# A dense FFN whose tail is reordered: chunks 0 to 5 of the last three blocks first, then chunks 6 to 15 of all blocks, mostly for 512 tokens at once

## The chip, the core and the metric

The kernel runs on one core of a Trainium2 chip. TensorE (PE, with its weight loads shown apart as PEld), VectorE (DVE), ScalarE (ACT), GpSimd (POOL) and the issuing engine SyncE (SP) each work through their own instructions in order and wait for each other through semaphores. The metric is the time of one execution on the device in microseconds (us); lower is better.

## What is computed

Three layers follow each other on 2304 tokens of 512 features (4 batches of 576):

```python
scores = scale * np.matmul(q, k.transpose(0, 1, 3, 2))      # 8 heads, head size 64
thresh = np.max(scores, axis=-1, keepdims=True) - tau
scores = np.where(scores >= thresh, scores, -1000000000.0)  # softmax over what is left, then @ v
...
h = x @ w_in                        # 512 x 2048
g = np.maximum(0.01 * h, h)
x = (g @ w_out).astype(np.float32)  # 2048 x 512
...
logits = x @ w_gate + modality_bias[modality_id]
e_idx = np.argmax(logits, axis=1)   # one of 8 experts for each token
for e in range(E):
    h = np.maximum(x[mask] @ w1[e], 0.0)
    out[mask] = gate_w[mask, None] * (h @ w2[e])
```

The weights of the dense FFN come as 64-bit floats.

## The kernel before, in words

**Precision by splitting.** Every f32 operand of a large matmul is kept as a high part (rounded to fp32r) and a low part (the rest), and three products are added: high by high, high by low, low by high. `mm1` does the first FFN product for one chunk of 128 hidden features: 4 slices of the 512 inputs, 3 products each, 12 matmuls into one PSUM bank `h`. `leaky` is the activation: ACT copies `h`, DVE takes the maximum, ACT rounds the high part `gh`, DVE subtracts to get `gl`. `mm2` adds the chunk's contribution to the output `y` of 128 tokens: 3 matmuls of 512 columns.

**Blocks, chunks, items.** A block is 256 tokens (`GT`), nine of them; a chunk is 128 of the 2048 hidden features, sixteen of them (`NF`). One block with one chunk is an item: 12 matmuls of 256 columns, a `leaky` on 256 columns, 6 matmuls of 512 columns. The input of a block comes from DRAM (`xd`, written by attention) into the one buffer `ur`, is transposed on PE (`turned`, 8 transposes into two PSUM tiles `tp`) and split by ACT and DVE (`split_x`).

**Weight conversion.** `convs` turns a piece (half a chunk, 128 by 512 double words) into a high and a low tile in four steps: ACT reads the upper words and DVE the lower ones, two more DVE operations put the bits together, then ACT writes the high part and POOL subtracts the low part. The intermediate `s` of the three DVE operations lies in PSUM (tile `cs`) for the first `NBANK` = 9 pieces and in SBUF for the other 23.

**Order of the work.** In the attention stage (16 head pairs with 9 row tiles, 144 steps) PE has room, and `Units` runs partial blocks there: blocks 0 to 5 with chunks 0 to 5 (`FB`, block 0 only chunks 0 to 4), whose sums go to DRAM as `yp` (issued by SP) and are added later. `CV` is the number of conversion steps for each attention step, by quarters of the stage. The partial block of the end also transposes and splits the input of the block that the tail starts with. After attention `un.finish` runs what is left of the units, and then `Tail.run` goes through a list of items: chunks 5 (or 6) to 15 of blocks 0 and 1 interleaved with a shift of two chunks (`AHEAD`), then chunks 6 to 15 of blocks 2 to 5, then all 16 chunks of blocks 6, 7 and 8, then two groups of the mixture of experts (8 items each). `pre` holds what has to be done ahead of an item (fetching an input, its transposes, loading and splitting expert weights). Within each item four conversion steps of `bg` are recorded, and `advance` takes one step of the routing work in `extra`. The matmuls of an item's `mm2` come two items after its `mm1` (`LAG`), and `h` has two banks.

**Routing.** When a block's output is complete (`done1`), the gate logits are computed on DVE (`Route.logits`: 16 fused multiply-and-sum operations of 512 columns a block against broadcast gate weights, which lie in the buffers of the expert weights), for the last block on PE (`logits_mm`: 8 transposes and 16 small matmuls). `Route.block` then finds the expert; five small matmuls `rp` on PE rank the tokens, the rows go to DRAM as `yd`, and POOL scatters the token numbers. `RB` and `LD` say how many calls of `advance` lie between two steps of them. `early` picks the first two expert groups from the blocks routed so far, here seven; their weights may be loaded (`have` = 2) when the eighth block is routed.

```python
RB = [4]*6+[3,3,1]
FB = [5,6,6,6,6,6]
CV = [0.95,0.67,0.67,0.67,0.67]
```

The names that the steps below use: `convs` (L369), `leaky` (L426), `Route.logits` (L533), `logits_mm` (L542), `Route.block` (L560), `Tail.run` (L918), the attention's stores of `xd` (L259, L262), the units' store of `yp` (L1276), the load of a block (L398).

Of the kernel before, what the change touches and what calls it, by code (L numbers as in the profile page):

```python
# [350 lines left out]
class Moe1:  # L351
# [17 lines left out]
    def convs(self, fs, new, tmp, bank, nbank):  # L369
# [7 lines left out]
        for n, (fi, k) in enumerate(seq):  # L377
# [3 lines left out]
            if n < nbank:  # L381
                s = bank().bitcast(I32)
# [31 lines left out]
def mm1(nc, w, x, h):  # L414

    n = 0
    for c in range(4):
# [4 lines left out]
        if c == 1:  # L422
            yield
# [299 lines left out]
class Steps:  # L723
# [9 lines left out]
    def to(self, k):  # L733
        while True:
            next(self)
            if self.n % 4 == k:
                return

# [9 lines left out]
class Tail:  # L748

# [6 lines left out]
    def __init__(self, tc, ctx, mo, rt, un, w1, w2, out, wts):  # L756
# [26 lines left out]
        self.pr = un.ps  # L783
        self.yT = [f(un.ct[i]).rearrange("p (c t) -> p c t", c=4) for i in (2, 0)]
# [14 lines left out]
    def turn(self, key, rows, t):  # L799
        if t == 0:  # L800
            self.xs = self.xh(), self.xl()
        else:
            self.x[key] = self.xs
        tp = self.pr.tile([P, 4, P], F32, tag="u", name="tp")
        turned(self.tc.nc, rows[:, t], tp, self.rt.ident)
        for _ in split_x(self.tc.nc, tp, *self.xs, t):
            pass

    def done1(self, b, ys, part):
        nc = self.tc.nc  # L810
        yt = self.yt()
        for t in range(2):
            if part:
# [9 lines left out]
        if self.blocks < NB:  # L823
# [20 lines left out]
    def load_ids(self, g):  # L844
        assert self.blocks == NB - 2
# [5 lines left out]
    def gather(self, g):  # L851
        xg, ids, rows = self.xgb(), self.idb(), self.rt.yd[0:NT - 2 * GT]
        self.tc.nc.vector.tensor_scalar(ids, self.ids[g], NT - 2 * GT - 1, None, op0=ALU.min)
# [64 lines left out]
    def run(self, items, pre, bg=None):  # L918
# [24 lines left out]
        for n in range(len(items) + self.LAG):  # L943
            if n < len(items):
# [10 lines left out]
                h = self.ph()[:, 0:GT]  # L955
                for _ in mm1(nc, w, self.x[it["x"]], h):
                    for _ in late:
                        pass
                    if bg:
                        bg.to(2)  # L960
                    self.advance()
                if bg:
                    bg.to(3)
                self.advance()
                gs[n] = self.g()
                if it["act"] is relu:
                    relu(nc, h, *gs[n])
                else:
                    late = leaky(nc, h, self.ga(), *gs[n])
# [6 lines left out]
            if n >= self.LAG:  # L976
                it = items[n - self.LAG]
                if it["start"]:
                    ys[it["y"]] = [self.py() for t in range(2)]
                g = gs.pop(n - self.LAG)  # L980
                for t in range(2):
                    mm2(nc, it["wt"], g, ys[it["y"]][t], t, it["start"], it["stop"])
                    if t == 0:
# [4 lines left out]
            if bg:  # L988
                bg.to(0)
# [207 lines left out]
RB = [4]*6+[3,3,1]  # L1197
# [6 lines left out]
FB = [5,6,6,6,6,6]  # L1204
CV = [0.95,0.67,0.67,0.67,0.67]
AHEAD = 2
NBANK = 9
# [3 lines left out]
class Units:  # L1211
# [32 lines left out]
    def block(self, b):  # L1244
# [18 lines left out]
        if b == len(FB) - 1:  # L1263
            yield from self.split(self.part[0])
        for t in range(2):
# [258 lines left out]
```

## Time and profile before

| | |
|---|---|
| median of 3 runs | 1050.35 us (1049.22 to 1051.45) |
| the profiled execution | 1050.26 us, its span 1048.5 us |
| mean granted TensorE clock | 0.963 |
| PE busy / PEld / DVE / ACT / POOL | 89% / 79% / 74% / 57% / 41% of the span |
| attention with units | to about 400 us |
| tail of the FFN, to the first matmul of expert group 0 | about 400 to 768 us |
| expert groups and the rest | 768 us to the end |

The span runs from the first instruction to the last; the execution's own time is 1.76 us more. A row of the timeline gives the start, the busy time, the engine, the line, the operation with out<-in, the count of merged instructions and, in brackets, the idle time before it with what ended it. Matmuls of one row overlap, so the spacing between starts tells how fast PE goes, and the busy time of a row does not.

### The profile page before, as it was taken

What the parts mean: (1) busy time and instruction counts of PE and PEld (TensorE: products, weight loads), DVE (VectorE), ACT (ScalarE), POOL (GpSimd) and SP (SyncE); (2) the same over time, 40 slices, a digit from 0 to 9 for tenths busy, and PEclk for the clock granted to TensorE, in tenths of its full rate; (3) what the DMA queues carried; (4) which work ended last, traced back from release to release, by engine and by line L of the source; (5) the groups of instructions that cost most, each with busy time, mean ns of one, the idle gap of its engine ahead of it and who ended that gap; (6) DMA issues with size and microseconds to landing.
All of it is one profiled execution on the core that took longest, in us unless ns stands there. A gap on an engine that the chain in (4) does not pass through costs nothing. (4 is left out here: it accounts for less than half of the span.)

```text
span 1048.5 us, 21500 instructions
## 1 busy us (share of the span) xinstructions
PE 929.8 (89%) x7409; PEld 827.5 (79%) x7409; DVE 780.8 (74%) x1975; ACT 595.6 (57%) x1234; POOL 430.9 (41%) x514
## 2 busy tenths in 40 slices
PE   4677789989998998778999999999899999999983
PEld 4566678879897997667888888988788998998962
DVE  7998999979898986786777877666458666565573
ACT  6778888878887874443222232322345555564473
POOL 3999999897887862331000000000102211221121
PEclk9888899999999999999999999999989999999997
DMA  8999999999999896444022221100756988665573
GB/s 220 197 241 236 242 238 219 197 212 232 208 186 240 184 180 181 125 156 137 24 62 61 45 37 41 41 22 1 147 196 167 351 292 267 242 234 170 158 262 114
DMA packets 260336, 177.33 MB, mean 169 GB/s; under 512 B 186018, under 2 KB 223014, under 8 KB 260200
## 3 DMA queue, kind: packets, MB, share of 16 engines
q1 hardware_dynamic: 251744, 160.53, 62.7%
q0 software_dynamic: 4736, 12.92, 3.8%
q10 hardware_dynamic: 3720, 2.22, 0.7%
q8 instruction: 65, 1.06, 0.5%
q14 instruction: 71, 0.58, 0.2%
HBM read 115.74 MB, written 18.22 MB: 128 GB/s over the span
## 5 line engine op out<-in xcount | busy, mean ns | idle before, releaser
L452 PE MATMUL y<-w,g 128*128 128x512 f32 x960 | 259.4, 406 | 0.0
L452 PEld LDWEIGHTS y<-w,g 128*128 128x128 f32 x960 | 172.8, 192 | 29.5
L420 PE MATMUL h<-uxh,w 128*128 128x256 f32 x848 | 166.6, 293 | 19.7 <-POOL w L393 7.0
L196 POOL TENSOR_TENSOR p<-p,p 128x512 f16<-128x512 f32 x144 | 169.0, 1173 | 0.0
L420 PEld LDWEIGHTS h<-uxh,w 128*128 128x128 f32 x848 | 137.1, 193 | 33.7 <-DVE g L434 11.9
L150 PE MATMUL s<-khh,qs 128*128 128x288 f32 x320 | 107.3, 348 | 48.5 <-DVE p L175 24.8
L158 DVE TENSOR_REDUCE s<-s 128x1 f32<-128x576 f32 x144 | 109.4, 760 | 29.7 <-PE s L223 26.0
L432 ACT ACTIVATE g<-h 128x256 fp32r<-128x256 f32 x144 | 55.4, 384 | 133.9 <-DVE h L430 131.9
L604 POOL DMA_INDIRECT idt<-ids,pi x18 | 18.7, 1041 | 263.9 <-DVE pi L601 197.9
L420 PE MATMUL h<-uxl,w 128*128 128x256 f32 x424 | 121.3, 286 | 0.7 <-DVE uxl L411 0.7
L175 DVE SCALAR_TENSOR_TENSOR p<-s,tb,e 128x576 f32<-128x576 f32 x144 | 117.3, 815 | 5.6 <-ACT e L167 3.9
L150 PEld LDWEIGHTS s<-khh,qs 128*128 128x128 f32 x320 | 68.1, 213 | 57.8 <-DVE p L175 18.1
L222 PE MATMUL s<-vs,pt 128*128 128x128 bf16 (+1 forms) x680 | 108.5, 227 | 5.7 <-DMA pt<-p 5.7
L428 ACT ACTIVATE ct<-h 128x256 f32<-128x256 f32 x144 | 55.2, 383 | 102.1 <-PE h L420 96.3
L167 ACT ACTIVATE e<-s,tb 128x576 f32<-128x576 f32 x144 | 107.2, 744 | 5.2 <-DVE tb L162 5.2
L223 PE MATMUL s<-vs,pt 128*128 128x64 bf16 (+1 forms) x680 | 103.5, 197 | 0.0
L430 DVE SCALAR_TENSOR_TENSOR h<-h,ct 128x256 f32<-128x256 f32 x144 | 61.7, 429 | 54.5 <-ACT ct L428 53.8
L194 ACT ACTIVATE p<-p 128x576 f16<-128x576 f32 x144 | 99.4, 691 | 3.7 <-DVE kll L111 2.9
L150 PE MATMUL s<-kll,qs 128*128 128x288 f32 x320 | 98.6, 321 | 0.0
L225 PE MATMUL s<-vs,pt 128*128 128x128 bf16 (+1 forms) x544 | 89.1, 225 | 0.0
L420 PE MATMUL h<-exh,w 128*128 128x256 f32 (+1 forms) x448 | 85.8, 287 | 0.7 <-ACT exh L409 0.7
L420 PEld LDWEIGHTS h<-uxl,w 128*128 128x128 f32 x424 | 81.7, 193 | 1.1 <-DVE uxl L411 1.1
(236 smaller groups left out, 2267.7 us busy)
## 6 DMA issues: line engine op xcount, KB each, us to landing
cr<-w SPq DMA_DIRECT2D x36, 512.0 KB, 6.0
raw_qk<-qkt SPq DMA_DIRECT2D x30, 576.0 KB, 5.3
raw<-w SPq DMA_DIRECT2D x24, 512.0 KB, 6.7
eraw<-w SPq DMA_DIRECT2D x18, 512.0 KB, 5.3
cr<-w_in SPq DMA_DIRECT2D x16, 512.0 KB, 4.2
cr<-w_out SPq DMA_DIRECT2D x16, 512.0 KB, 4.2
ur<-xd SPq DMA_DIRECT2D x15, 512.0 KB, 5.1
ur<-w SPq DMA_DIRECT2D x12, 512.0 KB, 3.6
```

The costliest lines, as they stand in the source:

```text
L150: nc.tensor.matmul(s[:, j, 0:288], qf[:, c0:c0 + P], x[:, j * 288:(j + 1) * 288], start=(k == 0), stop=(k == len(ops) - 1))
L158: v.tensor_reduce(self.mq[n], self.sq[n], axis=AX.XY, op=ALU.min)
L167: self.tc.nc.scalar.activation(e, self.sq[n], AF.Exp, bias=self.mq[n][:, 1:2], scale=-1.0)
L175: self.tc.nc.vector.scalar_tensor_tensor(p, self.sq.pop(n), self.mq.pop(n)[:, 0:1], self.eq.pop(n), op0=ALU.is_le, op1=ALU.mult, accum_out ...
L194: nc.scalar.activation(pp[:, 0:S], p, AF.Copy)
L196: nc.gpsimd.tensor_tensor(pp[:, S + D:], p[:, 0:4 * P], pp[:, 0:4 * P], op=ALU.subtract)
L222: nc.tensor.matmul(o[r0:r1, 0:2 * D], hi, v12, start=(c == 0), stop=False)
L223: nc.tensor.matmul(o[r0:r1, D:2 * D], hi, vs[:, h, c, 2], start=False, stop=(c == 4))
L225: nc.tensor.matmul(o[r0:r1, 0:2 * D], pt[:, 5 + c, r0:r1], v12, start=False, stop=False)
L420: nc.tensor.matmul(h, w[:, 0, a, s], b[:, c], start=(n == 0), stop=(n == 11))
L430: nc.vector.scalar_tensor_tensor(h, h, 0.01, a, op0=ALU.mult, op1=ALU.max)
L452: nc.tensor.matmul(y, a[:, s], w[:, 1, b], start=start and k == 0, stop=stop and k == 2)
```

## The change

It reorders the tail, and moves some work into and out of the attention stage:

- Block 0 gets chunk 5 in the attention stage as well (`FB`), and the conversions run faster in its first quarter (`CV` 1.2). The partial block at the end no longer transposes and splits the tail's first input.
- The tail starts with chunks 0 to 5 of blocks 6, 7 and 8 (18 items of 256 tokens), which need no new weights; their sums go to `yp` (`done0`). Then come chunks 6 to 15 of block pairs 0 and 1, 2 and 3, 4 and 5, 6 and 7 with 512 tokens an item (40 wide items; four `y` banks, inputs and activations in the weight tiles of chunks 0 to 5, which are not needed any more), then chunks 6 to 15 of block 8 (10 items).
- Three conversion steps are recorded in an item of 256 tokens and five in a wide one. `s` lies in PSUM until the first wide item, and in SBUF after it.
- The stores of `yp` are issued by ACT, and not by SP. The partial sums of a pair are loaded in the middle of the pair into their own buffers.
- Logits on DVE for the first six blocks only; on PE for the last three. `RB` is 1 for all blocks. `early` and `have` = 2 come after six blocks, and the gather reads only their rows.

```diff
-    def convs(self, fs, new, tmp, bank, nbank):
+    def convs(self, fs, new, tmp, bank):
...
-            if n < nbank:
-                s = bank().bitcast(I32)
+            at = bank()
+            if at is not None:
+                s = at.bitcast(I32)
...
-def mm1(nc, w, x, h):
+def mm1(nc, w, x, h, at=(1,)):
...
-        if c == 1:
+        if c in at:
             yield
...
+        self.x5 = itertools.cycle([[w.rearrange("p a b n -> p (a b) n") for w in wts[2 * i:2 * i + 2]] for i in range(2)]).__next__
+        self.g5 = itertools.cycle([[w[:, i, k] for k in range(2)] for w in wts[4:6] for i in range(2)]).__next__
+        self.a5 = itertools.cycle([f(t) for t in un.ct[0:2]]).__next__
...
+    def done0(self, b, ys):
+
+        for t in range(2):
+            o = f(self.cts[2 * t])
+            self.tc.nc.scalar.activation(o, ys[t], AF.Copy)
+            self.tc.nc.scalar.dma_start(self.mo.yp[2 * b + t], o)
+
+    def fetch_part(self, b):
+        for t in range(2):
+            self.tc.nc.sync.dma_start(self.xgs[b % 2][:, t, 0:DM], self.mo.yp[2 * b + t])
...
+            if part == 2:
+                nc.vector.tensor_tensor(yt[:, t, 0:DM], ys[t], self.xgs[b % 2][:, t, 0:DM], op=ALU.add)
+            elif part:
...
-        if self.blocks < NB:
+        if self.blocks == 1:
+            self.extra.append(iter([None] * 12))
+        if self.blocks <= NB - 3:
             self.extra.append(slowly(self.rt.logits(yt, self.sb, f(self.cts[2])), LD[self.blocks - 1]))
...
-        if self.blocks == NB - 2:
+        if self.blocks == NB - 3:
             self.extra.append(self.rt.early(self.sb1))
-        elif self.blocks == NB - 1:
             self.extra.append(self.routed())
...
-                for _ in mm1(nc, w, self.x[it["x"]], h):
+                if "hook" in it:
+                    it["hook"]()
+                nt = it.get("nt", 2)
+                h = self.ph()[:, 0:nt * P]
+                for _ in mm1(nc, w, self.x[it["x"]], h, (0, 1, 2) if nt == 4 else (1,)):
                     for _ in late:
                         pass
                     if bg:
-                        bg.to(2)
+                        next(bg)
                     self.advance()
...
-RB = [4]*6+[3,3,1]
+RB = [1] * 9
...
-FB = [5,6,6,6,6,6]
-CV = [0.95,0.67,0.67,0.67,0.67]
-AHEAD = 2
-NBANK = 9
+FB = [6,6,6,6,6,6]
+CV = [1.2,0.67,0.67,0.67,0.67]
...
-        if b == len(FB) - 1:
-            yield from self.split(self.part[0])
...
-                nc.sync.dma_start(mo.yp[2 * b + t], self.ys)
+                nc.scalar.dma_start(mo.yp[2 * b + t], self.ys)
...
+        bank[0] = itertools.cycle(ta.pys[2:4]).__next__
         un.finish(cv)
...
+        for b in range(len(FB), NB):
             p = len(items)
...
+            pre += [(p - 5, 0, 0, lambda b=b: ta.fetch(b))] + [(p - 2 + t, 0, 0, lambda b=b, t=t: ta.turn(b, un.xr, t)) for t in range(2)]
+            items += [item(b, fi, start=fi == 0, stop=fi == NA - 1, ys=ta.pys[0:2], done=(lambda ys, b=b: ta.done0(b, ys)))
+                      for fi in range(NA)]
...
+        for b in range(0, NB - 1, 2):
+            p = len(items)
+            for k in range(2):
+                pre += [(p - 4 + 2 * k, 0, 0, lambda b=b, k=k: ta.fetch(b + k)), (p + 5, 0, 0, lambda b=b, k=k: ta.fetch_part(b + k))]
+                pre += [(p - 2 + k, 0, 0, lambda b=b, t=2 * k + t: ta.turn((b,), un.xr, t, True)) for t in range(2)]
+            items += [dict(item(b, fi, start=fi == NA, stop=fi == NF - 1, nt=4, done=(lambda ys, b=b: both(b, ys))), x=(b,))
+                      for fi in range(NA, NF)]
+        items[(NB - len(FB)) * NA]["hook"] = lambda: bank.__setitem__(0, lambda: None)
```

**Where attention ends, on SP.** `xd<-xs` and `xd<-xm` are the attention's last stores, `cr` the raw weights, `ur<-xd` the load of a block's input, `yp<-ct` the units' partial sums. Before:

```order
L1276 DMA yp<-ct_85 128x512
L259 DMA xd<-xs 128x4x128
L262 DMA xd<-xm 64x64 x2
L364 DMA cr_90<-w_in 128x4x256
L1276 DMA yp<-ct_85 128x512
L366 DMA cr_88<-w_out 128x1024
L398 DMA ur<-xd 128x2x512
```

With the change:

```order
L200 DMA_TRANSPOSE pt<-p_138 128x9x128
L259 DMA xd<-xs 128x4x128
L262 DMA xd<-xm 64x64 x2
L364 DMA cr_90<-w_in 128x4x256
L399 DMA ur<-xd 128x2x512
L366 DMA cr_88<-w_out 128x1024
L399 DMA ur<-xd 128x2x512
```

The stores of `yp` are gone from this queue, and the first load of the tail is now block 6, some of whose rows are written by the two stores right ahead of it.

**An item in the middle of the tail, on PE.** Before (`xl` is the low part of the input, `w_7119` and so on a chunk's weights, `y_7109` and `y_7110` the two output banks):

```order
L420 MATMUL h_7106<-xl,w_7119 128x256
L452 MATMUL y_7109<-w_7117,g 128x512 x3
L452 MATMUL y_7110<-w_7117,g 128x512 x3
L420 MATMUL h_7105<-xh,w_7120 128x256 x2
L420 MATMUL h_7105<-xl,w_7120 128x256
```

With the change (`w_70` and `w_71`, once the weights of chunks 2 and 3, hold the input's two parts, and `w_73` an activation):

```order
L421 MATMUL h_7125<-w_71,w_7141 128x512
L453 MATMUL y_7127<-w_7139,w_73 128x512 x3
L453 MATMUL y_7128<-w_7139,w_73 128x512 x3
L453 MATMUL y_7129<-w_7139,w_73 128x512 x3
L453 MATMUL y_7130<-w_7139,w_73 128x512 x3
L421 MATMUL h_7126<-w_70,w_7142 128x512 x2
L421 MATMUL h_7126<-w_71,w_7142 128x512
```

A wide item has as many matmuls of the first product as a narrow one, of twice the columns, and twice as many of the second.

**Routing of a block, on DVE.** `hot` is the one-hot expert, which `rp` on PE reads; `rk` reads `rp`. Before:

```order
L584 TENSOR_TENSOR hot<-w_605,fe 128x16
L434 TENSOR_TENSOR g<-h_7105,g 128x256
L430 SCALAR_TENSOR_TENSOR h_7106<-h_7106,ct_86 128x256
L591 TENSOR_REDUCE g<-ex 128x2
L593 TENSOR_TENSOR rk<-rp,cnt 128x16
```

With the change:

```order
L539 SCALAR_TENSOR_TENSOR ct_87,lw<-yt_91,cr_89 128x512 x2
L539 SCALAR_TENSOR_TENSOR ct_87,lw<-yt_91,cr_90 128x512 x2
L435 TENSOR_TENSOR w_72<-h_7126,w_72 128x512
L572 TENSOR_TENSOR lg<-lw,bsel 128x16
L574 TENSOR_REDUCE mx<-lg 128x2
L577 TENSOR_TENSOR oh<-lg,mx 128x16
L578 TENSOR_TENSOR lg<-lg,mx 128x16
L579 TENSOR_TENSOR oh<-oh,w_612 128x16
L583 TENSOR_REDUCE fe<-oh 128x2
L585 TENSOR_TENSOR hot<-w_612,fe 128x16
L592 TENSOR_REDUCE g<-ex 128x2
L594 TENSOR_TENSOR rk<-rp,cnt 128x16
```

The steps of the routing now follow each other without the activation work of an item between `hot` and `rk`, so the five `rp` matmuls come sooner after `hot` in PE's order.

## Rows read from the trace of the kernel before

**Rows 1.** Stretches: us, busy by engine (x instructions), PEclk, DMA share, GB/s.

```profile
425.00:450.00 25.00, 21.48 (x121) 18.50 (x120) 20.25 (x33) 11.26 (x26) 8.48 (x6) 0.91 0.42 131
450.00:475.00 25.00, 20.26 (x109) 16.94 (x109) 21.26 (x32) 11.05 (x27) 8.49 (x7) 0.91 0.42 139
...
756.00:761.00 5.00, 0.27 (x2) 0.30 (x3) 0.24 (x1) 0.00 (x0) 0.00 (x0) 0.83 0.75 112
761.00:766.00 5.00, 5.00 (x19) 4.42 (x18) 2.23 (x4) 1.91 (x4) 0.00 (x0) 0.50 0.74 269
```

**Rows 2.** Timeline of PE in a stretch without idle time.

```profile
629.50 1.56 PE L452 MATMUL y<-w,g 128*128 128x512 f32 x6
630.90 0.40 PE L420 MATMUL h<-uxh,w 128*128 128x256 f32 x2
...
632.33 1.54 PE L452 MATMUL y<-w,g 128*128 128x512 f32 x6
```

**Rows 3.** Timeline of PE from the end of attention to the first logits.

```profile
400.06 7.21 PE L452 MATMUL y<-w,g 128*128 128x512 f32 x30
407.11 0.40 PE L420 MATMUL h<-uxh,w 128*128 128x256 f32 x2
...
414.73 1.12 PE L404 MATMUL tp<-ident,ur 128*128 128x128 f32 x4 [4.58 <-DMA ur<-xd]
...
424.49 0.39 PE L420 MATMUL h<-uxh,w 128*128 128x256 f32 x1 [1.45 <-POOL w L393]
...
498.44 0.50 PE L420 MATMUL h<-uxh,w 128*128 128x256 f32 x2 [3.46 <-DVE g L434]
```

**Rows 4.** Timeline of PE where expert group 0 begins.

```profile
760.73 1.09 PE L404 MATMUL tp<-ident,xg 128*128 128x128 f32 x4 [5.43 <-DMA xg<-yd,ids]
761.47 2.91 PE L452 MATMUL y<-w,g 128*128 128x512 f32 x6
764.17 0.63 PE L420 MATMUL h<-uxh,w 128*128 128x256 f32 x2
...
766.49 0.60 PE L404 MATMUL tp<-ident,xg 128*128 128x128 f32 x4
...
768.33 0.40 PE L420 MATMUL h<-xh,w 128*128 128x256 f32 x2
```

**Rows 5.** The attention's last output on DVE, then SP's timeline after it.

```profile
400.61 0.28 DVE L254 SCALAR_TENSOR_TENSOR xs<-s,rs,xs 128x64 f32<-128x64 f32 x1 [1.86 <-ACT xs L251]
...
403.76 0.35 SPq L1276 DMA_DIRECT2D yp<-ct  x1
404.24 0.36 SPq L259 DMA_DIRECT2D xd<-xs  x1
404.95 1.10 SPq L262 DMA_DIRECT2D xd<-xm  x2
```

**Rows 6.** Time from issue to landing: the stores of L262, then the loads of L398.

```profile
DMA to landing us min/median/max: 2.1/4.9/7.0
...
DMA to landing us min/median/max: 3.9/5.1/9.6
```

**Rows 7.** Conversion on DVE by line: ns min/median/max; s in PSUM (cs), then SBUF.

```profile
L388 DVE SCALAR_TENSOR_TENSOR cs<-cr,cs x9: 680/684/689, 16.8 to 106.2; 128x512 int32<-128x512 int32 x9
L388 DVE SCALAR_TENSOR_TENSOR yt<-cr,yt x20: 691/1648/1671, 401.3 to 478.8; 128x512 int32<-128x512 int32 x20
```

**Rows 8.** Timeline of DVE while logits run: two starts of the activation, one item apart.

```profile
559.62 0.43 DVE L430 SCALAR_TENSOR_TENSOR h<-h,ct 128x256 f32<-128x256 f32 x1
559.96 0.68 DVE L538 SCALAR_TENSOR_TENSOR ct<-yt,raw 128x512 f32<-128x512 f32 x1
...
562.98 0.43 DVE L430 SCALAR_TENSOR_TENSOR h<-h,ct 128x256 f32<-128x256 f32 x1
```

**Rows 9.** Timeline of PE in the logits of the last block.

```profile
781.00 1.85 PE L557 MATMUL lp<-wg,ct 128*128 128x8 f32 x16
```

**Rows 10.** SP's issues of yp (ns); PE's waits for transposed attention weights, 150 to 400 us.

```profile
L1276 SPq DMA_DIRECT2D yp<-ct x12: 338/444/548, 171.6 to 408.0; - x12
...
PE s L222 <- DMA pt<-p: 4.6, 3, 3.6
```

More of the change, by code (lines that the diff above doesn't have):

```diff
@@ L731, in __next__ @@
         return next(self.gen, None)
[L733 to L737, printed above, removed]
 def slowly(gen, k):
@@ L844, in load_ids @@
     def load_ids(self, g):
-        assert self.blocks == NB - 2
+        assert self.blocks == NB - 3
         base = self.entry(g, 1, NID - GT)
@@ L968, in run @@
                 else:
-                    late = leaky(nc, h, self.ga(), *gs[n])
+                    late = leaky(nc, h, (self.a5 if nt == 4 else self.ga)(), *gs[n])
                     next(late)
@@ L977, in run @@
                 it = items[n - self.LAG]
+                nt = it.get("nt", 2)
                 if it["start"]:
-                    ys[it["y"]] = [self.py() for t in range(2)]
+                    ys[it["y"]] = it["ys"] if "ys" in it else [self.py() for t in range(nt)]
                 g = gs.pop(n - self.LAG)
-                for t in range(2):
+                for t in range(nt):
                     mm2(nc, it["wt"], g, ys[it["y"]][t], t, it["start"], it["stop"])
-                    if t == 0:
+                    if t < nt - 1:
                         self.advance()
@@ L988, in run @@
             if bg:
-                bg.to(0)
+                next(bg)
             self.advance()
@@ L1296, in ev @@
                         self.turn(self.todo[0])
-                    elif b == len(FB) - 1:
-                        self.turn(self.part[0])
                 yield
@@ L1412, in body @@
         ta.sb2 = lambda: groups().sb
+        bank[0] = itertools.cycle(ta.pys[2:4]).__next__
         un.finish(cv)
-        part = un.part
-        full = [b for b in range(NB) if b not in part]
-        jobs = [(b, FB[b]) for b in part[2:]] + [(b, 0) for b in full]
-        def item(b, fi, f0):
-            return dict(x=b, w=(lambda: mo.w[fi]), act=leaky, y=b, start=fi == f0, stop=fi == NF - 1, need=2 * fi + 1,
-                        done=(lambda ys: ta.done1(b, ys, f0 > 0)))
-        b0, b1 = part[:2]
@@ L1422, in body @@
-        two = sorted([(fi, 0, b0) for fi in range(FB[b0], NF)] + [(fi + AHEAD, 1, b1) for fi in range(FB[b1], NF)])
-        items = [item(b, fi - (AHEAD if k else 0), FB[b]) for fi, k, b in two]
-        pre = []
-        ta.x[b0] = un.xh, un.xl
-        ta.xh(), ta.xl()
-        p = [it["x"] for it in items].index(b1)
-        pre += [(p - 9, 0, 0, lambda: ta.fetch(b1))] + [(p - 3 + t, 0, 0, lambda t=t: ta.turn(b1, un.xr, t)) for t in range(2)]
-        for b, f0 in jobs:
-            p = len(items)
-            pre += [(p - 9, 0, 0, lambda b=b: ta.fetch(b))] + [(p - 3 + t, 0, 0, lambda b=b, t=t: ta.turn(b, un.xr, t)) for t in range(2)]
-            items += [item(b, fi, f0) for fi in range(f0, NF)]
+        items, pre = [], []
@@ L1433, in body @@
+        items[(NB - len(FB)) * NA]["hook"] = lambda: bank.__setitem__(0, lambda: None)
+        b, p = NB - 1, len(items)
+        pre += [(p - 4, 0, 0, lambda: ta.fetch(b))] + [(p - 2 + t, 0, 0, lambda t=t: ta.turn((b,), un.xr, t)) for t in range(2)]
+        items += [dict(item(b, fi, start=fi == NA, stop=fi == NF - 1, done=(lambda ys: ta.done1(b, ys, 1))), x=(b,)) for fi in range(NA, NF)]
         p = len(items)
```

28 lines of the change are left out of this document (16 added, 12 removed).

## The prediction

> **What bounds the kernel now.** The stretches come first, since the 89% of the whole span hides them. From 425 to 475 us PE is busy 41.7 of 50 us, at a granted clock of 0.91 [rows 1]: it has work and waits for it. Next, the rate of PE when nothing holds it: an item takes 632.33 - 629.50 = 2.83 us, 1.40 for the six matmuls of `y` and 1.43 for the twelve of `h` [rows 2]; I count 2.82. A matmul of 512 columns so takes 0.233 us and one of 256 columns 0.119: width itself gains nothing on PE. Then the tail against that rate. From its first matmul (407.11) to the first of group 0 (768.33) lie 361.2 us [rows 3, 4]. In it are 109 items less the two `y` parts that come later, 109 x 2.82 - 2.8 = 304.6, and the transposes of nine inputs at 0.44 for four (766.49 to 768.33 is 1.84, less 1.40 for the `y` matmuls between) [rows 4], 7.9. So 48.7 us are lost: at 414.73 to a load (4.58), then to weights in conversion (1.45 at 424.49 is one of twelve such rows to 480), at 498.44 to the first logits (3.46), at 760.73 to the gather for group 0 (5.43) [rows 3, 4]. After an idle stretch PE is slow as well: at 0.50 of the clock, the lower of the two levels, from 761 to 766 [rows 1], the `y` part takes 2.70 for 1.40 and the `h` part 2.32 for 1.41 [rows 4], which with the transposes makes 2.6 us.
>
> The DVE rows say why weights are late: the second operation of a piece takes 1.65 us with `s` in SBUF, 0.68 with it in PSUM [rows 7].
>
> **The change part by part**, as the new time of group 0's first matmul.
>
> *Start of the tail.* The units leave 21 `y` matmuls after attention's last product for the 30 that fill 400.06 to 407.11: 4.9 us, so PE is free at 405.0 [rows 3]. But the first input is now block 6, which needs attention's last stores. Their data are ready at 400.9; SP issues them at 404.24 and 404.95 because the store of `yp` ahead of them waits until 403.76 [rows 5]. Without it the three issues take until 402.5, the last at about 402.0. Landing takes 4.9 (2.1 to 7.0), then the load is issued (0.4) and takes 5.1 (3.9 to 9.6) [rows 6]: 412.4. Transposes 0.88 and, as an estimate, two passes of ACT and DVE over 512 columns at about 0.68 each [rows 7]: first matmul at 414.7. PE is idle for most of 9.7 us, longer than at any place before; I take the 2.6 us of slow clock behind it.
>
> Here a rule speaks against the change. The Trainium skill (DMA: Bandwidth & Descriptors, Issuing engines are not separate DMA queues) says that issuing from several engines saves only the sequencer's time of issue. By it the start would come 3 us later, 417.7. The trace disagrees in that a queue's wait counts as well: 3.3 us passed between ready data and issue [rows 5], so I keep 414.7.
>
> *Narrow items.* 18 x 2.82 = 50.8. Their weights are there already. Conversion goes on at 3 steps, 0.75 pieces, an item: on DVE 0.75 x 3 x 0.68 = 1.5, with 0.43 twice for the activation [rows 8] 2.4 us, under the 2.82 of PE. With `s` in SBUF it would be 0.7 more, over it. For queues that meet I take 2 us; the bounds are 0 and the 12 us lost between 425 and 475 (8.3 idle, and 0.09 of 41.7 to the clock) [rows 1].
>
> *Wide items.* 40 x 5.64 = 225.6, the same PE time as 80 items. One loading buffer serves both blocks of a pair: the second load can start only after the first block's transposes. Before the first pair the two are one narrow item apart, so 5.1 + 0.4 - 2.8 = 2.7 us are lost; at the others a wide item covers it.
>
> *Logits.* On DVE four logits and an activation take 562.98 - 559.62 = 3.36 us [rows 8]. A wide item has room for eight: about 6.5 us of DVE work against 5.64 of PE, for 32 logits in a row instead of 16, after four additions at the pair's end. So DVE falls behind by some 0.9 us an item for two items, beside about 1 from the additions. PE has 8.5 us from a wide `h` to the reuse of its bank, so the activation bears that. The `rp` matmuls don't: they stand in PE's queue one step behind `hot`, where before there were four, and the next items' matmuls are queued behind them. For each of the six blocks I take 1.5 us, 9 in all; bounds 0 (DVE gets there first) and 4 each, all of the lag with the next additions.
>
> *Block 8 and more.* 10 x 2.82 less 2.8 = 25.4. Inputs: eleven more to transpose, and group 0, 12 x 0.88 = 10.6. Two more blocks have logits on PE: 0.88 + 1.85 = 2.7 each [rows 9], 5.4. Rank matmuls 1.8, small waits 1. The gather for group 0 and its weights are ready some items early, since six blocks are enough: the 5.43 us go [rows 4], and so does the wait for the first logits, whose gate weights get 12 steps to arrive.
>
> Sum: 50.8 + 225.6 + 25.4 + 10.6 + 5.4 = 317.8; lost 2.6 + 2 + 2.7 + 9 + 1.8 + 1 = 19.1. From 414.7 this makes 751.6 against 768.33: **-16.7 us**. The groups behind it keep their own work and order, so they count as nothing; what covers them is that their loads start as many items ahead as now.
>
> *Attention.* Nine conversion steps, 2.25 pieces, move from the second quarter to the first: at most +4.6 us (2.25 x 3 x 0.68, all of it on the path), at best -6 (as many pieces at the SBUF price less in the second). Twelve issues of `yp` move to ACT: at most +5.3 (12 x 0.444), at best -4.6, PE's waits for transposes that SP issued late [rows 10]. Block 0's chunk adds 2.8 of PE work, and a split of 0.9 goes; PE idles at the end of each quarter, so 0 to +1.9. I take **+1.5**, in the middle, as the costs and the gains fall on the same engines.
>
> 1050.26 - 16.7 + 1.5 = **1035.0 us**. The profiled execution lies 0.09 us under the median of the runs shown, so nothing is to be corrected.
>
> **The rivals.** (A) *DVE keeps up.* The `rp` cost nothing: 1026. For it: in a pair of 56 us DVE has 10 x 1.4 us of activation and 32 x 0.67 of logits, 35 us, so that it is early again by the pair's end. Against it: the 3.46 at 498.44 shows that logits in the queue do stop PE [rows 3]. (B) *Attention pays.* Both upper bounds, +9.9 instead of +1.5: 1043.4. (C) *Slower: PE stands behind `rp` for whole stretches of logits.* If DVE is late by the work of an item and not by a part of it, each `rp` costs 6.5 us; six make 39 instead of 9: 1065. It decides from 4.4 us each, (9 + 15.3 + 2.1) / 6, the last being the 0.2%. For it: 32 logits in one row, which the kernel before never had. Against it: PE's wait lets DVE catch up, so one long wait shortens the next. (D) *The reordering doesn't free the narrow items:* they still wait on the activation behind conversion, and the 12 us stay: 1045.
>
> **How the numbers follow.** Chances: forecast 0.50, A 0.22, B 0.13, C 0.08, D 0.07. The range goes from A with attention 4 better, 1022, to B with D's half, 1047; C and the worst of B with D lie above it. No change, within 0.2% (2.1 us, about what a measurement of this kernel can tell), needs B and D together or a half of C: 0.06. Slower is C: 0.08. Faster is the rest, 0.86.
>
> **What would show it.** Right: PE busy over 23 of 25 us from about 420 on, at clock 1.00; no wait on POOL or ACT for weights; no gap ahead of group 0's transposes; one gap of 8 to 10 us after attention ended by the load of `ur`; a wait of 2 to 3 us ahead of the first pair; six waits of 1 to 2 us at `rp`. Wrong: `rp` waits over 4 us each; attention's last product later than 406 us; gaps between narrow items; or an idle start much longer than 10 us.

## The result and the profile after

| | before | after |
|---|---|---|
| median of the runs | 1048.58 us (20 runs, 1043.75 to 1051.45) | 1055.68 us (20 runs, 1045.21 to 1063.01) |
| ratio to before, 95% interval | | 1.0052 (1.0027 to 1.0077) |
| profiled execution, its span | 1050.26, 1048.5 us | 1056.48, 1054.8 us |
| mean granted TensorE clock | 0.963 | 0.955 |
| group 0's first matmul | 768.33 | 765.36 |
| from there to the end of the span | 280.2 us | 289.4 us |

The forecast was 1035.0 us, with a range of 1022 to 1047. The kernel became **slower by half a per cent**. The ratio compares the fast runs alone (their means are 1053.9 and 1048.4), without the run of 1063.01, which was in a slower state. The stretches tell where it did what was expected of it, and where not. The windows of the kernel after, with the columns of [rows 1]:

```profile
425.00:450.00 25.00, 23.67 (x153) 21.05 (x152) 19.49 (x39) 15.30 (x35) 7.74 (x6) 1.00 0.52 174
450.00:475.00 25.00, 23.66 (x142) 20.77 (x141) 18.05 (x35) 14.42 (x32) 7.79 (x6) 1.00 0.54 181
475.00:500.00 25.00, 25.00 (x110) 20.27 (x109) 16.89 (x24) 11.81 (x21) 6.76 (x5) 1.00 0.37 127
...
550.00:650.00 100.00, 90.53 (x392) 72.28 (x391) 71.00 (x214) 20.59 (x39) 8.09 (x8) 0.93 0.27 49
...
656.00:662.00 6.00, 5.20 (x17) 4.45 (x18) 1.98 (x3) 1.68 (x3) 0.00 (x0) 0.50 0.01 4
```

The stretch that was bad before, 425 to 475 us, is good now: PE is busy 47.3 of 50 us at full clock, where it was 41.7 at 0.91 [rows 1]. But from 550 us on, where the kernel before had nothing to lose (98.9 of 100 us from 550 to 650, clock 1.00), PE now idles a tenth of the time (busy 90.5 of 100 us) and the mean granted clock is 0.93. The timeline of PE shows each loss:

```profile
399.28 5.12 PE L453 MATMUL y<-w,g 128*128 128x512 f32 x21
409.05 1.67 PE L405 MATMUL tp<-ident,ur 128*128 128x128 f32 x8 [4.65 <-DMA ur<-xd]
411.41 0.80 PE L421 MATMUL h<-uxh,w 128*128 128x256 f32 x2 [0.69 <-ACT uxh L410]
...
466.66 1.07 PE L405 MATMUL tp<-ident,ur 128*128 128x128 f32 x8 [1.34 <-DMA ur<-xd]
...
580.17 0.21 PE L590 MATMUL rp<-hot,tri 128*128 128x8 bf16 x2 [2.64 <-DVE hot L585]
...
617.43 0.20 PE L590 MATMUL rp<-hot,tri 128*128 128x8 bf16 x2 [2.67 <-DVE hot L585]
...
617.57 4.59 PE L453 MATMUL y<-w,w 128*128 128x512 f32 x12
622.00 2.96 PE L421 MATMUL h<-w,w 128*128 128x512 f32 x12
...
656.80 1.94 PE L405 MATMUL tp<-ident,ur 128*128 128x128 f32 x8 [5.04 <-DMA ur<-xd]
...
759.72 1.05 PE L405 MATMUL tp<-ident,xg 128*128 128x128 f32 x4
...
765.36 0.40 PE L421 MATMUL h<-uxh,w 128*128 128x256 f32 x2
...
779.48 1.11 PE L548 MATMUL ytp<-ident,yt 128*128 128x128 f32 x4 [6.82 <-DVE yt L827]
```

Three kinds of wait are new.

**The rank matmuls `rp`.** Six blocks wait 2.43, 2.64, 2.67, 1.73, 2.67 and 1.69 us, 13.8 in all. (A seventh wait, of 1.79 at 757.10, belongs to the fourth pair.) Behind the wait of 2.67 at 617.43 the twelve matmuls of `y` take 622.00 - 617.57 = 4.43 us, where they take 2.80 at full clock. That is 1.6 us more. The first four waits are followed by such a stretch, 6.4 us in all, the last two aren't. With it the six cost 20.2 us. Windows right behind the waits of 580.17, 636.40 and 690.63:

```profile
580.30:583.00 2.70, 2.70 (x11) 2.15 (x10) 1.43 (x8) 0.04 (x1) 0.95 (x1) 0.50 0.84 301
...
636.50:641.00 4.50, 4.50 (x19) 3.56 (x19) 2.22 (x9) 1.19 (x2) 0.96 (x1) 0.67 0.32 118
690.70:695.00 4.30, 4.30 (x23) 3.53 (x24) 3.95 (x16) 0.70 (x2) 0.96 (x1) 1.00 0.66 186
```

**The second input of the fourth pair.** It is waited for 5.04 us at 656.80, and the granted clock behind it is 0.50, the lower of its two levels, in the window of 656 to 662 above: 7.5 us with the 2.5 that this costs the transposes and the `y` matmuls. There was no such wait in this stage before, and the forecast had none here.

**Block 8's partial sums.** At 779.48 PE waits 6.82 us for the output of block 8. SP's issues, and behind them the addition on DVE, tell why:

```profile
759.56 0.38 SPq L880 DMA_DIRECT2D raw<-w  x1
766.11 0.37 SPq L878 DMA_DIRECT2D raw<-w  x1
...
767.20 0.89 SPq L826 DMA_DIRECT2D yt<-yp  x2
```

```profile
778.74 1.41 DVE L827 TENSOR_TENSOR yt<-y,yt 128x512 f32<-128x512 f32 x2 [6.49 <-DMA yt<-yp]
```

The load of `yp` is issued behind two expert weights, one of which stood in the queue until 766.11 for its buffer. It then takes until 778.7 to arrive, while expert weights and, on POOL from 775.05, a token scatter and two gathers are under way. This is the stretch after group 0's first matmul, which the forecast gave nothing.

What DVE does ahead of the `rp` of 580.17:

```profile
577.14 0.18 DVE L572 TENSOR_TENSOR lg<-lw,bsel 128x16 f32<-128x16 f32 x1
...
577.44 0.69 DVE L431 SCALAR_TENSOR_TENSOR h<-h,ct 128x512 f32<-128x512 f32 x1
578.04 1.28 DVE L412 TENSOR_TENSOR w<-tp,w 128x512 fp32r<-128x512 f32 x2
579.24 0.17 DVE L577 TENSOR_TENSOR oh<-lg,mx 128x16 f32<-128x16 f32 x1
...
579.93 0.17 DVE L585 TENSOR_TENSOR hot<-w,fe 128x16 bf16<-128x16 f32 x1
```

The last logit is done at 577.1, before PE came to `rp` (580.17 - 2.64 = 577.53). What PE then waits for here is not logits: it is an activation and the split of the next pair's first input, 1.7 us, and a chain of small operations, 0.9, which all stand ahead of `hot` in DVE's order. Read the same way, the 13.8 us of the six waits are 7.2 of that chain, 3.5 of activations, 1.2 of this one split, and only 1.9 of logits still running (at three of the six).

### The profile page after: what moved, and what is told of

The parts are those of the page before. It is cut to its first block, busy times and chain, and to the rows that moved or that the text cites. A ratio compares the mean times of both kernels' runs of the same rounds, so it can differ in the third digit from the quotient of the medians.

```text
span 1054.8 us, 20411 instructions
## 1 busy us (share of the span) xinstructions
PE 935.5 (89%) x7001; PEld 816.3 (77%) x7001; DVE 744.8 (71%) x1842; ACT 587.7 (56%) x1165; POOL 428.6 (41%) x514
## 5 line engine op out<-in xcount | busy, mean ns | idle before, releaser
L429 ACT ACTIVATE ct<-h 128x256 f32<-128x256 f32 (+1 forms) x104 | 48.3, 465 | 150.1 <-PE h L421 146.6
L453 PE MATMUL y<-w,g 128*128 128x512 f32 x480 | 130.3, 407 | 0.0
L431 DVE SCALAR_TENSOR_TENSOR h<-h,ct 128x256 f32<-128x256 f32 (+1 forms) x104 | 55.3, 532 | 97.8 <-ACT ct L429 97.5
L453 PE MATMUL y<-w,w 128*128 128x512 f32 x480 | 124.3, 410 | 0.0
L421 PE MATMUL h<-w,w 128*128 128x512 f32 x480 | 120.4, 399 | 0.0
L453 PEld LDWEIGHTS y<-w,w 128*128 128x128 f32 x480 | 93.6, 197 | 20.9
L421 PEld LDWEIGHTS h<-w,w 128*128 128x128 f32 x480 | 91.3, 191 | 21.6 <-DVE w L412 0.2
L453 PEld LDWEIGHTS y<-w,g 128*128 128x128 f32 x480 | 85.6, 191 | 14.2
L421 PE MATMUL h<-uxh,w 128*128 128x256 f32 x448 | 88.6, 296 | 0.7 <-ACT uxh L410 0.7
```

The lines of the kernel that those rows point to most:

```text
L421: nc.tensor.matmul(h, w[:, 0, a, s], b[:, c], start=(n == 0), stop=(n == 11))
L431: nc.vector.scalar_tensor_tensor(h, h, 0.01, a, op0=ALU.mult, op1=ALU.max)
L453: nc.tensor.matmul(y, a[:, s], w[:, 1, b], start=start and k == 0, stop=stop and k == 2)
```

## The experiments

The theory after this reading: the slowdown is the sum of three mishaps that have nothing to do with wide items as such, an `RB` that is too short, one loading buffer for two inputs, and a load that is issued too late. The rivals: wide items make DVE late whatever `RB` is; the loads are slow from contention and a buffer more doesn't help; or what is mended in one place is waited for in the next. The first three kernels are the change with one edit each, the fourth has all three. Microseconds under or over another kernel are the difference of the two ratios, times 1049; each reading of a trace is of one profiled execution.

**Block 8's partial sums early.** They are loaded into an idle weight tile four items into block 8, and added from there.

```diff
+        pre += [(p + 4, 0, 0, lambda: ta.fetch_last(b))]
...
-        items += [... done=(lambda ys: ta.done1(b, ys, 1)) ...]
+        items += [... done=(lambda ys: ta.done1(b, ys, 3)) ...]
```

> The changed kernel, but block 8's partial sums are loaded four items into block 8 (into a weight tile that is free then) and no longer at its end. Theory (the wait of 6.8 us for them and about 2.6 us of slow clock behind it are on the path): 8 to 9 us less than the changed kernel, ratio to the kernel before about 0.997. Rival 1 (expert group 0's weights are late anyway, so PE stops there for something else): 0 to 3 us less. Rival 2 (transfers next to the token scatter are slow whenever they are issued): the wait shrinks by less than half.

Measured: 1050.19 us, ratio 1.0005 (0.9976 to 1.0034), which is 4.9 us under the change, and not the 8 to 9 expected. The wait at `ytp` fell to 0.2, but about half of the gain was taken back. PE's row and POOL's rows ahead of it, in this kernel:

```profile
788.58 1.08 PE L405 MATMUL tp<-ident,xg 128*128 128x128 f32 x4 [5.49 <-issue]
```

```profile
776.21 0.96 POOL L605 DMA_INDIRECT idt<-ids,pi  x1 [12.87 <-DMA idt<-ids,pi]
777.47 0.98 POOL L874 DMA_INDIRECT xg<-yd,ids  x1 [0.30 <-PE h L421]
```

Group 1's gather (`xg`) stands in POOL's queue behind a token scatter of block 7 that waits 12.9 us for the landing of the scatter ahead of it. So this wait was there all along, hidden by the other.

**The rank matmuls three steps later.**

```diff
-RB = [1] * 9
+RB = [3] * 6 + [1] * 3
```

> The changed kernel with RB 3 instead of 1 for the first six blocks, so that three calls of advance and not one lie between hot on DVE and the rank matmuls on PE. Theory (PE stands behind the rank matmuls, 13.8 us in six waits, and loses 7 us to the clock behind them): 14 to 20 us less than the changed kernel, ratio about 0.988. Rival (DVE is behind by logits anyway, and the wait moves to the activation of the next item): under 5 us less, with PE waiting for DVE's g instead of hot.

Measured: 1039.69 us, ratio 0.9908 (0.9878 to 0.9939), 15.1 us under the change. PE's waits from 425 to 1000 us (total, count, longest), first of the change, then of this kernel:

```profile
PE rp L590 <- DVE hot L585: 15.6, 7, 2.7
```

```profile
PE tp L405 <- DMA ur<-xd: 7.2, 2, 5.8
...
PE rp L590 <- DVE hot L585: 1.8, 1, 1.8
```

The six waits are gone (the one left is the fourth pair's), so wide items don't keep DVE behind whatever `RB` is: three steps are enough, and the first rival falls. From attention's last product to group 0's first matmul the profiled run takes 20.7 us less (746.29 - 400.88 against 765.36 - 399.28), close to the 20.2 read from the rows of the six `rp`. The wait for the second input appears at another pair (5.82), so it was not an accident of one place.

**A buffer of its own for a pair's second input.**

```diff
+        self.xr2 = f(self.raws[1]).rearrange("p (t c) -> p t c", t=2)
...
-                pre += [(p - 4 + 2 * k, 0, 0, lambda b=b, k=k: ta.fetch(b + k)), ...]
+                pre += [(p - 4, 0, 0, lambda b=b, k=k: (ta.fetch2 if k else ta.fetch)(b + k)), ...]
```

> The changed kernel with a second buffer for the second input of each pair, both loaded four items ahead. Theory (one loading buffer leaves one item for the second load, which is on the path when the transfer is slow): 5 to 9 us less than the changed kernel, and less spread between runs; ratio about 0.998. Rival (the slow load at 657 us was an accident of the profiled run): under 2 us less.

Measured: 1051.88 us, ratio 1.0021 (1.0000 to 1.0042), 3.3 us under the change; the two intervals overlap, and 5 to 9 us were expected. No wait of over 0.7 us for an input of a pair is left in the tail after 425 us. Group 0 comes 8.1 us earlier after attention's last product, of which 2.9 go to a longer wait for block 8's sums (9.7 for 6.8). So the second rival falls as far as the wait goes; how much time the buffer is worth by itself stays open.

**All three.**

> The three edits together. Theory: they add up, 27 to 38 us less than the changed kernel, about 1020 us, ratio 0.973. Rival (each wait only hides the next): 10 us less at most, ratio 0.995.

Measured: 1032.33 us, ratio 0.9826 (0.9782 to 0.9870). The three gains add: 0.47, 1.44 and 0.31 make 2.22%, and together they are 2.26%, with an interval of 0.44 either way. That is 23.7 us, less than the 27 to 38 expected, since two of the three brought less than expected alone; but the gains add, so none of the three only hides another. The third rival is right beside them: what is left over 5 us is the start, and group 1's transposes (7.99 at 771.12), behind the same token scatters that the first edit had brought to light.

**Group 1's gather ahead of block 7's scatters.** Added to the three:

```diff
-        a = [..., (p - 7, 1, lambda: self.gather(g)),
+        a = [..., (p - 7 - 8 * g, 1, lambda: self.gather(g)),
```

> The three edits together, and the gather of the tokens of expert group 1 eight items earlier, so that on POOL it stands ahead of the token scatters of blocks 6 and 7 and no longer behind them. Theory (where the partial sums are early, PE waits 5 to 8 us for that gather, and POOL's scatters each wait for the one before): 7 to 10 us less than the three edits, ratio about 0.974. Rival (group 1's weights are as late as its tokens): under 3 us less, ratio 0.981.

Measured: 1038.14 us, ratio 0.9887 (0.9863 to 0.9910), a miss. Expected were 7 to 10 us less, and it is 6.4 more than with the three edits alone, with intervals that just touch. Group 1's wait is gone, but the next customer of the same chain now waits. The timelines of POOL, of SP and of PE in this kernel:

```profile
780.57 1.35 POOL L605 DMA_INDIRECT idt<-ids,pi  x1 [6.48 <-DMA idt<-ids,pi]
...
791.94 0.98 POOL L1060 DMA_INDIRECT exg<-yd,eid  x1 [7.18 <-DMA eid<-idt]
```

```profile
788.60 0.35 SPq L1054 DMA_DIRECT2D eid<-idt  x1
```

```profile
799.71 1.09 PE L405 MATMUL tp<-ident,exg 128*128 128x128 f32 x4 [9.62 <-DMA exg<-yd,eid]
```

Each scatter waits for the one before it to land, the list of tokens is read after the last one, and the first group of the table gathers after that. So, by these rows, the chain of scatters sets the groups' time, and moving one gather only chooses who waits; the next two kernels test it.

**The scatters freed of one another.** To the three edits: each token has a row of its own, so no scatter needs another's landing. The edit also puts a POOL operation on one column ahead of each, whose own effect was not tried.

```diff
-            nc.gpsimd.indirect_dma_start(out=self.idt, ...)
+            nc.gpsimd.memset(sb.tile([P, 1], F32, tag="z", name="z"), 0.0)
+            i = nc.gpsimd.indirect_dma_start(out=self.idt, ...)
+            self.tc.declare_no_dep(i.ins, group="idt", reason="every token has a row of its own")
+            self.tc.add_to_no_dep_group("idt", i.ins)
```

> The kernel with all three edits, and the eighteen token scatters (of ids into the sorted list) no longer wait for one another's landing; each has a row of its own to write. A one-column POOL fill stands ahead of each. If POOL's queue, held by one scatter's wait for the landing of the one before it, is what makes group 1's gather late, the scatters of block 7 are issued about 1 us apart, group 1's gather is issued some 10 us earlier, the wait of 7.99 us ahead of its transposes goes to under 1, and the ratio falls from 0.983 to 0.974 to 0.978. If instead the landing itself is slow because of loads beside it, the gather comes no earlier by more than 2 us and the ratio stays at 0.98 to 0.985.

Measured: 1022.85 us, ratio 0.9751 (0.9726 to 0.9777). POOL now issues block 7's two scatters 1.3 us apart, and group 1's gather at 749.55, 9.7 us earlier than with the three edits alone (759.26):

```profile
737.12 0.96 POOL L606 DMA_INDIRECT idt<-ids,pi  x1 [11.55 <-DVE pi L602]
738.38 0.96 POOL L606 DMA_INDIRECT idt<-ids,pi  x1 [0.19 <-issue]
749.55 0.97 POOL L881 DMA_INDIRECT xg<-yd,ids  x1 [10.21 <-DVE ids L879]
```

The wait of 7.99 is gone. The rival, slow landings from loads beside them, doesn't explain this, since the gather came earlier by far more than 2 us.

**Freed scatters and the early gather.** Both edits on top of the three.

> As the run before, and the gather of group 1 ahead of block 7's scatters, which by itself had cost 6 us because the first gather of the table's groups came late (a wait of 9.62 us). If that wait came from the chain of scatters of blocks 7 and 8, each behind the landing of the one before, it goes to under 3 us, and the ratio is 0.974 to 0.978, the same as of the run before. If it came from the table's own work or from the loads beside it, it stays over 6 us and the ratio is 0.985 to 0.99.

Measured: 1024.42 us, ratio 0.9759 (0.9734 to 0.9783). The wait of 9.62 us for the table's first gather is gone too, so it came from the scatters. Beside the run before, moving the gather does nothing that can be told from noise.

**The fourth pair's ranks a step later.** On top of the run before:

```diff
-RB = [3] * 6 + [1] * 3
+RB = [3] * 6 + [2, 2, 1]
```

> As the run before, and the rank matmuls of the fourth pair (blocks 6 and 7) two steps behind their logits and not one. The theory that one step is too short: the last wait for the hot vectors (1.79 us, and the slow clock behind it) goes, and the ratio is 0.002 to 0.004 lower than of the run before. The rival, that the later ranks make block 7's scatters and so the groups late: the wait goes and as much comes back at group 1 or at the table's first gather, and the ratio is the same within 0.002.

Measured: 1021.36 us, ratio 0.9732 (0.9707 to 0.9756), **the fastest of all**, 2.7% under the kernel before. The last wait for `hot` (1.8 us) is gone and none came for it; the gain of 0.27% is what was expected, but the intervals of the two runs overlap, so its size stays open. Its windows, and group 0 on PE:

```profile
475.00:550.00 75.00, 75.00 (x334) 61.13 (x333) 35.86 (x56) 25.36 (x45) 8.09 (x7) 1.00 0.32 113
550.00:650.00 100.00, 98.62 (x459) 79.64 (x458) 78.15 (x231) 24.67 (x46) 8.75 (x16) 1.00 0.20 43
650.00:734.00 84.00, 84.00 (x458) 71.32 (x457) 59.53 (x186) 21.66 (x46) 10.33 (x16) 1.00 0.39 95
```

```profile
739.28 0.48 PE L421 MATMUL h<-uxh,w 128*128 128x256 f32 x2
```

PE is busy 257.6 of 259 us through the wide stage, at full clock. From group 0's first matmul to the end it is 1019.4 - 739.28 = 280.1 us, what the kernel before takes (280.2).

**The kernel before with its scatters freed.** A control: how much of this gain is in that edit alone?

> The kernel before, with the token scatters freed of one another's landing and nothing else. It tells what of the best version's gain belongs to that edit alone. In the kernel before the gather for group 0 is issued at 749.04, 1.3 us after a scatter that waited 7.3 us for the landing of the one ahead: freed, the gather comes up to 7 us earlier and the 5.43 us at group 0 with the slow clock behind it go, 5 to 8 us or a ratio of 0.992 to 0.995. If the wait at group 0 comes from its ranks, not from the scatters, the ratio is 1.000. In both cases the order of the tail with wide items keeps most of its 2.7%.

Measured: 1050.18 us, ratio 1.0014 (0.9995 to 1.0033): none. The gather for group 0 comes 4.5 us earlier than before (744.51 for 749.04), the wait of 5.43 us for it is gone, and PE still idles at nearly the same place, for something else. ACT and PE of this kernel:

```profile
758.19 0.63 ACT L445 ACTIVATE w<-raw 128x512 fp32r<-128x512 f32 x1 [4.89 <-DMA raw<-w]
```

```profile
759.94 0.50 PE L420 MATMUL h<-uxh,w 128*128 128x256 f32 x2 [4.05 <-DVE g L434]
```

ACT stands at the conversion of an expert weight that was issued at 742.77 and hasn't landed, and the activation that PE needs is queued behind it. In the kernel before the same load, issued at 740.79, was converted at 750.71 without a wait. So in this kernel the wait has only moved from the gather to a weight; that the early gather is what made that load slow was not tried. The fastest version has neither wait: its gather for group 0 is issued at 716.82, 22 us ahead of the group.

**The kernel before with the short `RB`.**

```diff
-RB = [4]*6+[3,3,1]
+RB = [1]*9
```

> The kernel before with RB 1 for all blocks, nothing else. Theory (one step between hot and the rank matmuls makes PE wait, whatever the width of the items): waits of 1 to 2 us at the rank matmuls of eight blocks, 8 to 16 us slower than the kernel before, ratio 1.008 to 1.015. Rival (it is the 32 logits in a row and the wide items that make DVE late): under 3 us slower, ratio 1.002.

Measured: 1061.51 us, ratio 1.0123 (1.0102 to 1.0145). PE's waits from 425 to 1000 us:

```profile
PE rp L589 <- DVE hot L584: 14.0, 8, 2.0
```

Eight blocks wait 1.75 us each with items of 256 tokens, and the kernel loses 12.9 us. So the price of the short `RB` doesn't need wide items: in either kernel one step is too short for the chain that leads to `hot`.

**The stores of `yp` on SP again.** The change with that part undone:

```diff
-                nc.scalar.dma_start(mo.yp[2 * b + t], self.ys)
+                nc.sync.dma_start(mo.yp[2 * b + t], self.ys)
```

> The changed kernel with the attention stage's stores of yp issued by SP again. Theory of the prediction (a wait in SP's queue holds up attention's last stores and with them the first load of the tail): the tail's first matmul 2 to 4 us later after attention's last product, the whole 2 to 4 us slower than the changed kernel, ratio 1.008. Rival (only the time of issue moves between two sequencers): no difference beyond 1 us, ratio 1.005.

Measured: 1059.11 us, ratio 1.0085 (1.0057 to 1.0113). PE's wait at the start of the tail:

```profile
413.15 1.94 PE L405 MATMUL tp<-ident,ur 128*128 128x128 f32 x8 [6.92 <-DMA ur<-xd]
```

It is 6.92 us, against 4.65 in the change and 4.71 to 5.49 in the nine other runs of this list with the stores on ACT. So moving the stores is worth 1.4 to 2.3 us at the start, in one profile with them on SP; the whole difference of 0.33% (3.5 us) isn't clear of noise, as the two intervals overlap. SP's rows in this kernel:

```profile
406.94 0.34 SPq L1289 DMA_DIRECT2D yp<-ct  x1
407.38 0.37 SPq L399 DMA_DIRECT2D ur<-xd  x1
```

By the Trainium skill (DMA: Bandwidth & Descriptors, Issuing engines are not separate DMA queues), which grants another issuing engine only the sequencer's time of issue, the wait would have stayed the same but for one issue of 0.4 us; the trace shows more, as an issue that waits holds up what is queued behind it. But what it held up here was not attention's stores, as in the forecast: those went out at 403.28 and 404.01, as soon as their data were there. It was the load of block 6, which went out 2.3 us after the stores were issued, behind a store of `yp` that waited for its data, and 0.9 us after them in the change.

**`s` in SBUF for the whole tail.** The change with that part undone:

```diff
-        bank[0] = itertools.cycle(ta.pys[2:4]).__next__
+        bank[0] = lambda: None
```

> The changed kernel with the intermediate of the conversion in SBUF for the whole tail. Theory (the PSUM bank is what keeps DVE under PE's time in the narrow items): 18 items at about 0.1 to 0.3 us more, and waits of PE for DVE there, 2 to 6 us slower than the changed kernel, ratio 1.008. Rival (3 steps an item instead of 4, and weights that are there, are what frees the narrow items): no difference beyond 1 us.

Measured: 1059.09 us, ratio 1.0098 (1.0070 to 1.0125), 4.8 us over the change, with intervals that just overlap. The second DVE operation in this kernel (ns, min/median/max) and the narrow stage's window:

```profile
L389 DVE SCALAR_TENSOR_TENSOR yt<-cr,yt x20: 677/688/1672, 407.9 to 503.5; 128x512 int32<-128x512 int32 x20
```

```profile
425.00:475.00 50.00, 46.65 (x291) 41.23 (x289) 37.98 (x70) 28.31 (x63) 14.52 (x12) 0.97 0.50 163
```

With `s` in SBUF most of these operations take 0.69 us, as in PSUM, and not the 1.65 of the kernel before [rows 7]; both values occur with the same operands. PE is busy 46.7 of 50 us in this window at a granted clock of 0.97, against 47.3 at 1.00 with `s` in PSUM and 41.7 at 0.91 before. So most of what the narrow stage gained doesn't come from PSUM. It comes from the rest of the change there: the first 18 items need no new weights, and an item has three conversion steps and not four. The runs don't separate these two. And of the 4.8 us only some 2 lie in this window (0.7 idle, 1.4 by the clock): the same profile has a wait of 10.2 us for block 8's sums, where the change has 6.8.

What decides between the two values is in the traces, in POOL's rows. First the kernel before, POOL's subtraction of a low part and DVE's second operation; then the same two in the change, with `s` in PSUM:

```profile
429.78 1.35 POOL L393 TENSOR_TENSOR w<-yt,w 128x512 fp32r<-128x512 f32 x1 [2.09 <-ACT w L392]
430.01 1.67 DVE L388 SCALAR_TENSOR_TENSOR yt<-cr,yt 128x512 int32<-128x512 int32 x1
```

```profile
434.47 1.29 POOL L394 TENSOR_TENSOR w<-yt,w 128x512 fp32r<-128x512 f32 x1 [3.83 <-ACT w L393]
434.97 0.69 DVE L389 SCALAR_TENSOR_TENSOR y<-cr,y 128x512 int32<-128x512 int32 x1
```

In the kernel before, all 15 operations of 1.64 to 1.67 us after 400 us start 0.2 to 0.3 us after such a subtraction has started, and end 0.55 us after it has ended; the five of 0.69 to 0.70 start while POOL does none. In the kernel with `s` in SBUF it is the same: four of 20 start in that way and take 1.66 or 1.67. In the change, six with `s` in PSUM start during a subtraction and take 0.69 or 0.70 all the same. So the 1.65 is 0.69 and a wait for POOL's operation, which PSUM avoids, and which a SBUF operand meets only where the two fall together: 15 times of 20 in the order before, four of 20 in the order of the change.

## Why the prediction was wrong

**Right: the narrow and the wide items.** "18 x 2.82" and "40 x 5.64" hold: PE is busy 23.67 and 23.66 of 25 us from 425 on and all of 475 to 500, with no wait for weights. The reason given for the first was partly wrong. "With `s` in SBUF it would be 0.7 more, over it" took the 1.65 us as the price of SBUF. It is the price of starting while POOL subtracts, and the run with SBUF had a median of 0.69.

**Right: the start.** First matmul forecast at 414.7 plus 1.5 of attention, 416.2; it was 411.41 in the profiled run of the change, and 413.59 to 416.63 in eight other kernels with the same start. The distance from attention's last product was 12.1 to 13.2 us for a forecast of 14.6: the load went out at 404.40, 2.0 us after the issue of the last stores had begun, where the forecast had taken 4.9 for their landing. Attention itself ended between 399.28 and 404.92 in ten profiled runs with the same attention, forecast 401.6; before 400.06.

**Right: the gap at group 0.** "The gather for group 0 and its weights are ready some items early": there is no wait at 759.72, where there were 5.43 us [rows 4].

**Wrong in size, and in its reason: "For each of the six blocks I take 1.5 us, 9 in all".** They took 13.8 us of waiting and 6.4 of slow clock behind it, 20.2. The bound of 4 us each held (3.4), but it isn't only the size that was wrong. The forecast made the term from DVE's lag with 32 logits in a row. Logits still running were 1.9 us of the 13.8; the chain of small operations that ends in `hot` was 7.2, which one step of `RB` doesn't cover for any width of item, and activations and a split the rest. The kernel before with the short `RB`, and no wide item, loses 12.9 us. And the clock was charged behind the gap at the start and nowhere else.

**Wrong: "at the others a wide item covers it".** The second load of a pair can start only after the first one's transposes, one wide item of 5.64 us ahead. Landing takes 3.9 to 9.6 us [rows 6], so the cover holds for the median of 5.1 and fails for the long ones. At the fourth pair it was issued at 646.23 and waited for until 656.80, 10.6 us later, and the price was 7.5 us with the clock. The rows that warned of it were on the page; the forecast used only their median.

**Wrong: "The groups behind it keep their own work and order, so they count as nothing".** They took 289.4 us for 280.2. Block 8 is new among the blocks with partial sums in DRAM at the end of the tail, and its load of `yp` is issued when its output is complete, in SP's queue behind expert weights. The forecast counted the issues of the stores of `yp` one by one and missed the one load that comes late. That the stretch itself was unchanged is shown by the best version: 280.1 us once the load is early and the scatters don't wait.

The sum, in the profiled run: group 0 came at 765.36 for a forecast of 751.6 + 1.5 = 753.1, which is 12.3 us; the stretch behind took 9.2 more; together the 21.5 us between 1035.0 and 1056.5. Of the 12.3, the six `rp` cost 11.2 more than forecast and the fourth pair's load 7.5. The seventh `rp`, at 757.10, cost 3.5 us (its wait of 1.79, and 1.7 of slow clock behind it); the forecast had no term for it beyond "small waits 1". Attention and the start gave 4.8 back. That makes 17.4. The 5.1 us that are left were forecast and didn't come: 1.4 at the first pair (1.34 at 466.66 for 2.7), 0.7 of the 2 us for queues that meet in the narrow items, the 1 us of small waits, and, as an estimate, 2 in the work of PE itself, which without waits and slow clock comes to 317.6 us for 317.8 + 1.8.

**The rivals.** Rival C had the right place and the wrong point: it decides "from 4.4 us each", the `rp` cost 3.4 each, and what it lacked came from two places that were in no rival. Rival A (the `rp` cost nothing) was wrong for `RB` 1; three steps make the waits go. Against B, attention ended 2.3 us later in the mean of the ten runs than before (402.4 for 400.06), not 9.9; against D stand the narrow items, which lose 2.7 of 50 us and not 8.3.

## What to carry to other kernels

When work is moved, list for each value that crosses the moved border (a partial sum, an input, a rank) who loads it, in which queue, how late it is recorded, and what stands ahead of it; a stage that "keeps its own order" still inherits what the stage ahead of it now leaves to the end. A transfer is covered only if the cover is as long as its slow landings, and a wait of PE costs more than its length when the clock falls behind it. And where a wait is mended, look at the one behind it before counting the gain: here partial sums hid a gather, which hid a chain of scatters, and the chain's end brought 0.75% in one kernel and nothing in another.

## What the runs showed of the hardware

Short waits can bring the lower clock level as well: after a wait of 2.64 us (580.17) the granted clock was 0.50 from 580.3 to 583.0, and after 1.73 us at 636.40 it was 0.67 in the mean of the next 4.5 us. But after 2.67 us at 690.63 it stayed at 1.00, so the length of the one wait doesn't settle it; what does was not tried. The forecast had charged it only behind the long gap at the start.

A scatter of 128 single words from POOL is issued in 1 us, but the next one that has to wait for its landing goes 6.5 to 12.9 us later (the rows above), and as long as it waits everything behind it in POOL's queue waits too. Why the landing takes that long was not tried.

A DVE operation on two SBUF tiles that starts during a POOL subtraction of SBUF tiles waits for its end: 1.64 to 1.67 us instead of 0.69, in all 15 such cases after 400 us in the kernel before, by the times at which the two start and end. With one of the two tiles in PSUM it took 0.69 or 0.70 in the six cases of the change. The time of such an operation is so a matter of how two engines' orders meet, and a row with one number for it doesn't tell that.
